# A fused mLSTM, mixture-of-experts and gated-MLP kernel: the first expert's second layer for 256 rows moved ahead of a branch, and one read-back issued an expert earlier

## The chip, the cores and the metric

The kernel runs on one core of a Trainium2 chip. The metric is the device time of one execution in microseconds (us), taken as the median of several runs. Each engine of the core has its own instruction stream and works in order: TensorE (PE in the rows, its weight loads PEld) multiplies into PSUM, VectorE (DVE) and ScalarE (ACT) work element by element, GpSimd (POOL) does the same and issues the indirect transfers, SyncE (SP) issues all other DMAs. Engines wait for one another by semaphores.

## The reference, cut to what matters

```python
def _moe_ref(x, expert_emb, tau, w1, w2):            # x: 3072 tokens x 320, from the mLSTM
    expert_idx = np.argmax(logits, axis=1)            # one of 8 experts for each token
    gate_w = probs[np.arange(N), expert_idx]
    for e in range(E):
        mask = expert_idx == e
        h = np.maximum(x[mask] @ w1[e], 0.0)          # 320 -> 1024
        out[mask] = gate_w[mask, None] * (h @ w2[e])  # 1024 -> 320

def _moe2_ref(x, w_in, w_out):
    h = x @ w_in                                      # 320 -> 2048
    g = h * (1.0 / (1.0 + np.exp(-1.702 * h)))
    return g @ w_out                                  # 2048 -> 320
```

Ahead of it stands a recurrence over 768 time steps for 4 x 8 heads (`_attn_ref`), whose output, 3072 rows of 320 values, is `x` above.

## The kernel before, in words

The kernel has three phases on one core.

**Recurrence (about 0 to 195 us).** The 768 steps are cut into chunks of 128, and each of the 24 units (batch, chunk) becomes a few matmuls. As tokens come out, they are routed: each row is scattered to a slot of its expert in the DRAM tensor `rows`. The expert with most tokens so far is named early (`first`), its weights are loaded, and at the end of the phase the first 256 of its rows (`EARLY`) go through its first layer for the first six slices of 128 hidden units (`early_mm`, `early_relu`, `WA = 6`). The result of slice m is kept in `he[m]` as a high and a low part, in a buffer of the weight ring.

**A branch.** `order` computes on VectorE how many tokens each expert has, the order of the experts and a flag, which says whether any expert has more rows than its capacity, or the first one fewer than 256 among the early rows. Every engine loads the flag into a register (`values_load`, L1389) and takes `tc.If` (L1390). Where the flag is set, `general()` does the odd cases; with these inputs it is skipped. An engine that skips the block waits for its own semaphore to reach its count at the block's entry and then adds what the block would have added (the semaphore instructions on L1390). Behind the branch, work that touches what the block could have touched waits for those counts.

**Experts (about 199 to 412 us).** Each of the 8 experts, in order of size, is 8 slices (`m`) of 128 hidden units; `s` counts the 64 steps. A step runs the first layer of its slice (`h_mm`: eight matmuls with up to 512 columns, since operands are split into a high and a low part), `relu_split` (ScalarE the high part `hh`, VectorE the low part `hl`), and then the second layer of the slice before it (`tail` -> `o_mm`: three matmuls of 320 columns for each tile of 128 rows, accumulated in `acc`; those that need `hl`, one for each tile, come last). In the last slice of an expert (`m = 7`) the order is tile by tile, so `hl` is wanted by the third matmul. The step also splits a later weight slice (`split_w`: ScalarE L105 and L118, GpSimd L110, VectorE L111 and L121), transposes the next expert's rows (`prep_x`, `prep_x0` for the first expert) and advances the conversion of the gated MLP's weights, which arrive as 64-bit floats (`convert(n)` takes `n` steps of `cvt`: L1160, L1164, L1166, L1168, L1170 on VectorE). For the first expert, `prep_x0(1, c)` makes the rows 256 to 511 ready at once behind the branch, and `prep_x0(0, c)` the rows 0 to 255 in the steps 1 to 3, because slices 6 and 7 need them; in its steps 0 to 5 `h_mm` has 256 columns only, and `he[m]` supplies the other half. When an expert is done, `put` writes its rows to the DRAM tensor `y`.

**Gated MLP (about 412 to 772 us).** Blocks of 512 sorted rows are read back from `y` (`load_y`), scaled by the gate (`scale_y`), and go through both layers. The buffer `xr` that `load_y` fills has one copy, which the experts' rows use too. The first block's read-back is issued in the last expert's step `m == 1`, `scale_y` stands on VectorE at `m == 3`, and the transposes of the block at `m = 4` to `6`.

The order on every engine is that of the program text (`tc.manual_schedule()`); SyncE issues its DMAs in that order too, and one that has to wait holds all behind it.

Of the kernel before, what the change touches and what calls it, by code (L numbers as in the profile page):

```python
# [9 lines left out]
F32 = mybir.dt.float32  # L10
# [4 lines left out]
ALU = mybir.AluOpType  # L15
# [4 lines left out]
P = 128  # L20
CAP = 512

EARLY = 256
# [3 lines left out]
def kernel(ctx, tc, qT_in, kT_in, kvo_in, i_gate, f_gate, expert_emb, tau, w12, wio, out, dbg=None):  # L27

    nc = tc.nc
    B, H, S = i_gate.shape  # L30
    NT, DM = out.shape
    D = DM // H
    E = expert_emb.shape[0]
# [13 lines left out]
    RS = NT + GN  # L47
# [957 lines left out]
    with ExitStack() as mctx:  # L1005
# [16 lines left out]
        def load_x0(j):  # L1022

            if j:
                xr_t["first"] = xp.tile([P, NB, 3 * P], F32, tag="xr", name="xr", bufs=1)
                t = xr_t["first"][:, 0:NB // 2]
            else:
                t = mp2.tile([P, NB, DM], F32, tag="o", name="xr", bufs=1).rearrange("p i d -> p (i d)")
                t = t[:, 0:NB // 2 * 3 * P].rearrange("p (i d) -> p i d", d=3 * P)
            xr_t["first", j] = t  # L1030
            src = rows[ds(ids[0] * RS + j * EARLY, EARLY), :].rearrange("(i p) d -> p i d", p=P)
            nc.sync.dma_start(out=t[:, :, 0:DM], in_=src)

        def load_x(p):
            n = CAPS[p] // P
            xr_t[p] = xp.tile([P, NB, 3 * P], F32, tag="xr", name="xr", bufs=1)
            src = rows[ds(ids[p] * RS, CAPS[p]), :].rearrange("(i p) d -> p i d", p=P)
            nc.sync.dma_start(out=xr_t[p][:, 0:n, 0:DM], in_=src)
            nc.sync.dma_start(out=xr_t[p][:, 0:n, DM:3 * P], in_=src[:, :, 2 * P:DM])
# [45 lines left out]
        def halves(hh, hl):  # L1085
            return [(hh[:, i:i + P], hl[:, i:i + P]) for i in range(0, hh.shape[-1], P)]

        def relu_split(key, out=None):
            hp = hp_t.pop(key)
            nb = hp.shape[-1]  # L1090
            hh, hl = out or (mp2.tile([P, CAP], F32R, tag="hh", name="hh")[:, 0:nb], mp2.tile([P, CAP], F32R, tag="hl", name="hl")[:, 0:nb])
            nc.scalar.activation(out=hh, in_=hp, func=AF.Relu)  # L1092
            nc.vector.scalar_tensor_tensor(out=hl, in0=hp, scalar=0.0, in1=hh.bitcast(F32), op0=ALU.max, op1=ALU.subtract)  # L1093
            hs_t[key] = halves(hh, hl)
# [11 lines left out]
            nc.vector.tensor_tensor(out=hl, in0=g, in1=hh.bitcast(F32), op=ALU.subtract)  # L1106
            hs_t[key] = halves(hh, hl)

        def o_mm(blk, key, w, first, last):
            hs = hs_t.pop(key)  # L1110
            if first:
                acc_t[blk] = [ps_a.tile([P, DM], F32, tag="acc", name="acc") for _ in range(ncol(blk) // P)]


            n = ncol(blk) // P
            order_ = [(i, j) for i in range(n) for j in range(2)] + [(i, 2) for i in range(n)]
            for i, j in sorted(order_) if last else order_:
                hh, hl = hs[i]
                nc.tensor.matmul(acc_t[blk][i], hl if j == 2 else hh, w[:, DM:2 * DM] if j == 1 else w[:, 0:DM],  # L1119
                                 start=(first and j == 0), stop=(last and j == 2))  # L1120

        def out_tile(blk):
            o = mp2.tile([P, NB, DM], F32, tag="o", name="o", bufs=1)
# [113 lines left out]
        def load_y(blk):  # L1237
            n = ncol(blk)
            xg = xp.tile([P, NB, 3 * P], F32, tag="xr", name="xr", bufs=1)[:, 0:n // P]
            src = y[row0(blk):row0(blk) + n, :].rearrange("(i p) d -> p i d", p=P)  # L1240
            nc.sync.dma_start(out=xg[:, :, 0:DM], in_=src)
            nc.sync.dma_start(out=xg[:, :, DM:3 * P], in_=src[:, :, 2 * P:DM])
            xr_t[blk] = xg
# [42 lines left out]
            nc.scalar.copy(xh_t[blk][:, c, js], x)  # L1286
            nc.vector.tensor_tensor(out=xl_t[blk][:, c, js], in0=x, in1=xh_t[blk][:, c, js].bitcast(F32), op=ALU.subtract)  # L1287

        def general_x(src):
            xr_t["g"] = xr_t["first"][:, NB - GN // P:NB]  # L1290
            src = src.rearrange("(i p) d -> p i d", p=P)
            nc.sync.dma_start(out=xr_t["g"][:, :, 0:DM], in_=src)
            nc.sync.dma_start(out=xr_t["g"][:, :, DM:3 * P], in_=src[:, :, 2 * P:DM])
            for c in range(3):
                prep_x("g", c)

# [56 lines left out]
            return work, nc.values_load(nwork_i[0:1], min_val=0, max_val=NWK)  # L1353

        def general():
            general_x(rows[ds(ids[0] * RS, EARLY), :])
            for m in range(WA):
                h_mm("g", ("g", m), wslot[m][0])
                relu_split(("g", m), he[m])
                hs_t.pop(("g", m))  # L1360
            work, nwork = general_list()
            with tc.For_i(0, nwork, 1) as w:
                zero = mp2.tile([P, 3 * P], F32, tag="fr", name="zero")[:, 0:DM]
                nc.vector.memset(zero, 0.0)
                wt = mp2.tile([1, 4], I32, tag="wt", name="wt", bufs=1)
                nc.sync.dma_start(out=wt, in_=work[ds(w, 1)])
                e, r0, r1, y0 = (nc.values_load(wt[0:1, i:i + 1], engines=sp, min_val=0, max_val=m)
                                 for i, m in enumerate([E - 1, E * RS - GN, E * RS - GN, NT + CAP - GN]))
                nc.sync.dma_start(out=rows[ds(r1, GN), :].rearrange("(i p) d -> p i d", p=P), in_=zero.unsqueeze(1).to_broadcast([P, GN // P, DM]))
                general_x(rows[ds(r0, GN), :])  # L1370
                for m in range(0, M1, 2):
                    r = mp2.tile([P, 3 * P + DM, 2], I32, tag="c", name="c")
                    r1_, r2_ = w_dma(e, m // 2, r.bitcast(F32).rearrange("p w two -> p (w two)"))
                    for i in range(2):
                        split_w1(win[:, m + i], r1_[:, :, i * P:(i + 1) * P])
                        split_w2(wout[:, m + i], r2_[:, i])
                for m in range(M1):
                    h_mm("g", ("g", m), win[:, m])
                    relu_split(("g", m))
                    o_mm("g", ("g", m), wout[:, m], m == 0, m == M1 - 1)  # L1380
                for i, o in out_tile("g"):
                    pass
                nc.sync.dma_start(out=y[ds(y0, GN), :].rearrange("(i p) d -> p i d", p=P), in_=o[:, 0:GN // P])
# [2 lines left out]
        sp = [mybir.EngineType.SP]  # L1386
        with tc.manual_schedule():
            load_x0(1)
            flag = nc.values_load(vals_i[0:1, 2 * E:2 * E + 1], min_val=0, max_val=1)  # L1389
            with tc.If(flag > 0):  # L1390
                general()
# [26 lines left out]

            def tail(p):
                e, m, s = p  # L1420
                o_mm(e, ("a", s), wslot.pop(s)[1], m == 0, m == M1 - 1)
                if m == M1 - 1:
                    put(e)

            for e, m, s in steps:
                h_mm(e, ("a", s), wslot[s][0], EARLY if s in he else 0)
                relu_split(("a", s))
                if s in he:
                    hs_t["a", s] = halves(*he.pop(s)) + hs_t["a", s]
                if prev:  # L1430
                    tail(prev)
                prev = (e, m, s)
                if 1 <= s < 4:
                    prep_x0(0, s - 1)
                if s == 1:
                    gts = gates_1()
                if s == 2:
                    gates_2(*gts)
                if s == 3:
                    order_rows()  # L1440
                if s == 4:
                    meta_tile()

                for w in [] if s == 0 else [s + WA - 1] if s < WA else [s + WA - 1, s + WA] if s == WA else [s + WA]:
                    if w < NS1:
                        split_w(w)
                        if w % 2 and w // 2 + 3 < NS1 // 2:
                            load_w(w // 2 + 3)
                if e + 1 < E and 2 <= m - (e == 0) < 5:
                    prep_x(e + 1, m - 2 - (e == 0))  # L1450
                if m == 5 + (e == 0) and e + 2 < E:
                    load_x(e + 2)
                if s % 2 == 0 and 0 <= s // 2 - 3 < NTILE:
                    meta_put(s // 2 - 3)
                if s == 7 + 2 * NTILE:
                    meta_get()
                if s == 9 + 2 * NTILE:
                    meta_split()
                if e == E - 1:

                    if m == 1:
                        load_y(E)
                    if m == 3:
                        scale_y(E, nc.vector)
                    if 4 <= m < 7:
                        prep_x(E, m - 4)
                    if m == 7:
                        load_y(E + 1)

                if s > 3:  # L1470
                    convert((1 if CAPS[e] < CAP else 2) + (m % 4 > 0))

            def tail2(p):
# [102 lines left out]
```

## Time and profile before

| | |
|---|---|
| median of 3 runs | 773.79 us (773.63 to 774.51) |
| the profiled execution, its own time | 774.2 us |
| its span, first to last instruction | 772.5 us |
| mean granted TensorE clock | 0.985 |
| TensorE busy (matmuls) | 726.2 us, 94% of the span |
| VectorE, ScalarE, GpSimd busy | 560.0, 354.3, 248.0 us |

The 1.7 us between the span and the execution's own time lie around the span and are not part of the program. Busy matmul time is modelled and overlaps, so that 94% says that TensorE is seldom without work and not how fast it works. A granted clock of 1 is TensorE's upper level, 2.4 GHz, and one of 0.5 its lower, 1.2 GHz; a mean in between is a mix of both. Times in the rows are microseconds from the span's start.

### The profile page before, as it was taken

To read this page: it belongs to the slowest core of one execution; us is meant where nothing else is said; L and a number is where in the kernel's file an instruction comes from. 1 tells how busy PE (TensorE), PEld (TensorE's weight loads), DVE (VectorE), ACT (ScalarE), POOL (GpSimd) and SP (SyncE) were. 2 spreads that over 40 slices of the span, in tenths; PEclk is the share of its full clock that TensorE was granted. 3 is DMA by queue.
4 is the path that set the end of the run, shared out by engine and by line. 5 is a ranking of instruction groups with operands and counts; after the bars stand their busy time and mean duration, and the time that the engine had idled before them with its cause. 6 is when DMAs were issued, how large, how long until landed. Compare 5 with 4: busy or idle time off the path is not lost.

```text
span 772.5 us, 13249 instructions
## 1 busy us (share of the span) xinstructions
PE 726.2 (94%) x4708; PEld 678.3 (88%) x4708; DVE 560.0 (72%) x1146; ACT 354.3 (46%) x834; POOL 248.0 (32%) x362
## 2 busy tenths in 40 slices
PE   6798988879899999999989999999999999999995
PEld 6697988778889999999988888889889889989994
DVE  8888999998599989999977785554554554445542
ACT  4353424414465666666744554343333343334442
POOL 5564476785233434454511002002002002002011
PEclk9899999999999999999999999999999999999998
DMA  6979887752657765778633220120120110101000
GB/s 206 304 252 302 273 249 242 236 180 98 226 145 234 225 185 181 187 187 265 179 105 105 59 62 34 31 52 35 29 54 34 28 36 26 50 1 40 17 18 17
DMA packets 70302, 100.19 MB, mean 130 GB/s; under 512 B 31120, under 2 KB 56472, under 8 KB 70232
## 3 DMA queue, kind: packets, MB, share of 16 engines
q1 hardware_dynamic: 67160, 91.41, 39.9%
q0 software_dynamic: 3072, 7.89, 2.7%
q8 instruction: 38, 0.62, 0.4%
q14 instruction: 32, 0.26, 0.1%
HBM read 77.53 MB, written 17.82 MB: 123 GB/s over the span
## 4 chain that ended last, share of the span: by engine, by line
PE 45%; issue 20%; DVE 5%; POOL 2%; ACT 1%; POOLq 0%; ACTq 0%; DVEq 0%
PE hp L138 22%; PE acc L1119 21%; POOL out_dram L1141 2%; DVE w L121 1%; PE xt L1053 1%; DVE hl L1093 1%; POOL xr L1247 1%; DVE w L111 1%; DVE ex L1160 0%; DVE xl L1055 0%; DVE fr L1170 0%; DVE es L1168 0%; DVE sg L1104 0%; DVE fr L1166 0%; DVE hhl L1106 0%
## 5 line engine op out<-in xcount | busy, mean ns | idle before, releaser
L1119 PE MATMUL acc<-wout,hhl 128*128 128x320 f32 x1152 | 187.5, 310 | 0.1
L1119 PEld LDWEIGHTS acc<-wout,hhl 128*128 128x128 f32 x1152 | 175.9, 188 | 7.9 <-ACT o L1128 0.3
L1104 DVE TENSOR_TENSOR sg<-hp,sg 128x512 f32<-128x512 f32 (+1 forms) x112 | 68.7, 614 | 88.4 <-ACT sg L1103 88.3
L138 PE MATMUL hp<-xh,win 128*128 128x512 f32 (+1 forms) x560 | 131.1, 364 | 0.0
L1106 DVE TENSOR_TENSOR hhl<-sg,hhl 128x512 fp32r<-128x512 f32 (+1 forms) x112 | 71.4, 637 | 70.0 <-ACT hhl L1105 70.0
L1103 ACT ACTIVATE sg<-hp 128x512 f32<-128x512 f32 (+1 forms) x112 | 60.2, 538 | 115.4 <-PE hp L138 115.2
L1141 POOL DMA_INDIRECT out_dram<-o,tokd x24 | 24.0, 1000 | 273.6 <-ACT o L1128 269.9
L1105 ACT CAST hhl<-sg 128x512 fp32r<-128x512 f32 (+1 forms) x112 | 62.6, 559 | 91.0 <-DVE sg L1104 91.0
L138 PEld LDWEIGHTS hp<-xh,win 128*128 128x128 f32 x560 | 93.9, 188 | 11.5 <-ACT xh L1286 0.2
L138 PE MATMUL hp<-xl,win 128*128 128x512 f32 (+1 forms) x336 | 85.7, 363 | 0.0
L110 POOL TENSOR_TENSOR w<-r,w 128x256 fp32r<-128x256 f32 x58 | 46.4, 800 | 107.0 <-ACT w L105 106.6
L138 PE MATMUL hp<-xh,w 128*128 128x384 f32 (+2 forms) x320 | 75.7, 368 | 0.2 <-ACT xh L1070 0.2
L1119 PE MATMUL acc<-w,hh 128*128 128x320 f32 x424 | 75.6, 309 | 0.0
L1119 PEld LDWEIGHTS acc<-w,hh 128*128 128x128 f32 x424 | 67.7, 188 | 2.3
L138 PEld LDWEIGHTS hp<-xl,win 128*128 128x128 f32 x336 | 58.9, 189 | 10.8 <-DVE xl L1287 0.2
L360 DVE TENSOR_TENSOR_SCAN pm<-fb,ident_h 128x1024 f32<-128x1024 f32 x23 | 56.7, 2464 | 5.2 <-DMA fb<-dec 5.1
L400 PE MATMUL sp<-qT,kblk 120*128 120x128 f32 x384 | 50.8, 288 | 10.1 <-DVE wm L405 10.1
L400 PEld LDWEIGHTS sp<-qT,kblk 120*128 120x128 f32 x384 | 46.9, 200 | 14.7 <-DVE wm L405 12.7
L138 PEld LDWEIGHTS hp<-xh,w 128*128 128x128 f32 x320 | 55.1, 193 | 4.0 <-ACT xh L1070 0.4
L1092 ACT ACTIVATE hh<-hp 128x384 fp32r<-128x384 f32 (+2 forms) x64 | 33.5, 524 | 44.8 <-PE hp L138 43.8
L138 PE MATMUL hp<-xl,w 128*128 128x384 f32 (+2 forms) x192 | 47.9, 358 | 0.0
L1119 PE MATMUL acc<-w,hl 128*128 128x320 f32 x212 | 44.9, 310 | 1.5 <-DVE hl L1093 1.3
(305 smaller groups left out, 1219.2 us busy)
## 6 DMA issues: line engine op xcount, KB each, us to landing
r<-in_w_dram SPq DMA_DIRECT2D x32, 704.0 KB
fb<-dec SPq DMA_DIRECT2D x23, 512.0 KB
kvo<-in_kvo_dram SPq DMA_DIRECT2D x24, 480.0 KB
c<-in_wio_dram SPq DMA_DIRECT2D x16, 704.0 KB
rows<-zt SPq DMA_DIRECT2D x8, 640.0 KB
qT<-in_qT_dram SPq DMA_DIRECT2D x24, 180.0 KB
xr<-y SPq DMA_DIRECT2D x5, 640.0 KB
kblk<-in_kT_dram SPq DMA_DIRECT2D x48, 60.0 KB
```

The costliest lines, as they stand in the source:

```text
L110: eng.tensor_tensor(out=t[:, 3 * P:5 * P].rearrange("p (c f) -> p c f", c=2), in0=r1[:, 0:2], in1=hif[:, 0:2], op=ALU.subtract)
L111: nc.vector.tensor_tensor(out=hi[64:P, 2], in0=r1[64:P, 2], in1=hif[64:P, 2], op=ALU.subtract)
L138: nc.tensor.matmul(hp, a, b, start=(i == 0), stop=(i == len(seq) - 1))
L360: nc.vector.tensor_tensor_scan(out=pm[u].rearrange("p h t -> p (h t)"), data0=fb[u].rearrange("p h t -> p (h t)"), data1=ident_h.rearrange ...
L400: nc.tensor.matmul(sp[:, h - hs.start], kblk[u % NLD][0:KR, h // 3, h % 3, :], qT[u][0:KR, h // 3, :], start=True, stop=True)
L1092: nc.scalar.activation(out=hh, in_=hp, func=AF.Relu)
L1103: nc.scalar.activation(out=sg, in_=hp, func=AF.Sigmoid, scale=1.702)
L1104: nc.vector.tensor_tensor(out=g, in0=hp, in1=sg, op=ALU.mult)
L1105: nc.scalar.copy(hh, g)
L1106: nc.vector.tensor_tensor(out=hl, in0=g, in1=hh.bitcast(F32), op=ALU.subtract)
L1119: nc.tensor.matmul(acc_t[blk][i], hl if j == 2 else hh, w[:, DM:2 * DM] if j == 1 else w[:, 0:DM], start=(first and j == 0), stop=(last an ...
L1141: sc = nc.gpsimd.indirect_dma_start(out=out, out_offset=bass.IndirectOffsetOnAxis(ap=tokd[:, ti:ti + 1], axis=0), in_=o[:, i], in_offset=None)
```

## The change

There are three edits.

1. Ahead of the flag's load, the accumulators of the first expert's four row tiles are allocated, and `early_o` runs the second layer for the two early tiles and the six slices of `he`: 6 x 2 x 3 = 36 matmuls of 320 columns. In the expert's steps 1 to 6, `tail` then does tiles 2 and 3 alone for these six slices, six matmuls in place of twelve. Where the flag is set, `general()` computes these rows again; `late_rows` first clears those that were already counted, so that adding is right. That block's own accumulators move to the other PSUM pool.
2. `load_y(E)`, the read-back of the gated MLP's first 512 rows, is issued in step `m == 5` of the last but one expert and no longer in step `m == 1` of the last.
3. `convert` begins in step 5 and no longer in step 4.

```diff
-        def o_mm(blk, key, w, first, last):
-            hs = hs_t.pop(key)
-            if first:
-                acc_t[blk] = [ps_a.tile([P, DM], F32, tag="acc", name="acc") for _ in range(ncol(blk) // P)]
+        def o_mm(blk, key, w, first, last, tiles=None, hs=None):
+            hs = hs or hs_t.pop(key)
+            if first and blk not in acc_t:
+                acc_tiles(blk)
...
-            n = ncol(blk) // P
-            order_ = [(i, j) for i in range(n) for j in range(2)] + [(i, 2) for i in range(n)]
+            tiles = tiles or range(len(acc_t[blk]))
+            order_ = [(i, j) for i in tiles for j in range(2)] + [(i, 2) for i in tiles]
...
+        def acc_tiles(blk):
+            n = -(-ncol(blk) // P)
+            if blk == "g":
+                acc_t[blk] = [ps_x.tile([P, CAP], F32, tag="xt", name="acc")[:, 0:DM] for _ in range(n)]
+            else:
+                acc_t[blk] = [ps_a.tile([P, DM], F32, tag="acc", name="acc") for _ in range(n)]
+
+        NE = EARLY // P
+
+        def early_o(m, first):
+
+            o_mm(0, None, wslot[m][1], first, False, range(NE), halves(*he[m]))
+
+        def late_rows(x):
+
+            t = mp2.tile([P, 3 * P], F32, tag="fr", name="t")[:, 0:NE]
+            nc.vector.tensor_copy(t, tok_i[:, 0:NE])
+            nc.vector.tensor_scalar(out=t, in0=t, scalar1=lack, scalar2=None, op0=ALU.is_ge)
+            nc.vector.tensor_tensor(out=x, in0=x, in1=t.unsqueeze(2).to_broadcast([P, NE, 3 * P]), op=ALU.mult)
...
         def general():
-            general_x(rows[ds(ids[0] * RS, EARLY), :])
+            general_x(rows[ds(ids[0] * RS, EARLY), :], late_rows)
...
+            for m in range(WA):
+                early_o(m, False)
...
             load_x0(1)
+            acc_tiles(0)
+            for m in range(WA):
+                early_o(m, m == 0)
             flag = nc.values_load(vals_i[0:1, 2 * E:2 * E + 1], min_val=0, max_val=1)
             with tc.If(flag > 0):
                 general()
...
-                o_mm(e, ("a", s), wslot.pop(s)[1], m == 0, m == M1 - 1)
+                o_mm(e, ("a", s), wslot.pop(s)[1], m == 0, m == M1 - 1, range(NE, len(acc_t[0])) if s < WA else None)
...
                 if m == 5 + (e == 0) and e + 2 < E:
                     load_x(e + 2)
+                if m == 5 and e + 2 == E:
+                    load_y(E)
...
-                    if m == 1:
-                        load_y(E)
...
-                if s > 3:
+                if s > 4:
                     convert((1 if CAPS[e] < CAP else 2) + (m % 4 > 0))
```

## Rows read from the trace of the kernel before

**Rows 1.** TensorE's timeline around the branch: start, us, operation, count [idle before <-releaser].

```profile
194.99 0.52 PE L138 MATMUL hp<-xel,w 128*128 128x256 f32 x3
197.35 0.41 PE L1077 MATMUL xt<-ident 128*128 128x64 f32 x2 [1.84 <-DVEq L1390]
...
199.55 1.44 PE L138 MATMUL hp<-xh,w 128*128 128x256 f32 x5 [0.16 <-ACT xh L1070]
...
202.92 0.74 PE L1119 MATMUL acc<-w,he 128*128 128x320 f32 x4
...
204.66 0.38 PE L1069 MATMUL xt<-ident,xr 128*128 128x128 f32 x2
204.80 0.84 PE L138 MATMUL hp<-xh,w 128*128 128x256 f32 x5
...
205.84 0.75 PE L1119 MATMUL acc<-w,he 128*128 128x320 f32 x4
```

**Rows 2.** Records of the branch's line: engine, instruction, count, ns, first and last start.

```profile
L1390 SPq EVENT_SEMAPHORE  x9: 17/17/17, 196.3 to 198.6; - x9
L1390 PEldq EVENT_SEMAPHORE  x2: 51/51/51, 195.6 to 195.7; - x2
...
L1390 DVEq EVENT_SEMAPHORE  x2: 21/21/21, 197.2 to 197.3; - x2
```

**Rows 3.** SyncE's timeline: the first transfer issued behind the branch.

```profile
199.75 0.39 SPq L1032 DMA_DIRECT2D xr<-rows  x1
```

**Rows 4.** Busy time of each engine by stretch, granted clock, DMA share and GB/s.

```profile
200.00:205.00 5.00, 5.00 (x31) 5.00 (x31) 1.46 (x4) 1.00 (x4) 0.00 (x0) 0.74 0.76 234
...
210.00:215.00 5.00, 5.00 (x41) 4.99 (x40) 4.67 (x16) 3.41 (x9) 1.97 (x3) 1.00 0.69 248
215.00:220.00 5.00, 5.00 (x33) 4.63 (x32) 4.87 (x13) 3.22 (x8) 0.74 (x1) 1.00 0.44 146
```

**Rows 5.** TensorE's timeline in step 8.

```profile
228.38 0.42 PE L1119 MATMUL acc<-w,hl 128*128 128x320 f32 x1 [1.32 <-DVE hl L1093]
```

**Rows 6.** VectorE's timeline in the first expert's steps 1 to 7.

```profile
205.49 0.42 DVE L1071 TENSOR_TENSOR xl<-xt,xh 128x256 fp32r<-128x256 f32 x1 [1.48 <-ACT xh L1070]
...
208.34 0.29 DVE L111 TENSOR_TENSOR w<-r,w 64x128 fp32r<-64x128 f32 x1 [0.83 <-ACT w L105]
...
214.47 0.49 DVE L121 TENSOR_TENSOR w<-r,w 128x320 fp32r<-128x320 f32 x1
...
216.41 1.07 DVE L121 TENSOR_TENSOR w<-r,w 128x320 fp32r<-128x320 f32 x1
...
220.78 1.10 DVE L1168 SCALAR_TENSOR_TENSOR es<-c,es 128x384 int32<-128x384 int32 x1
...
226.26 0.29 DVE L111 TENSOR_TENSOR win<-fr,win 64x128 fp32r<-64x128 f32 x1
226.56 0.33 DVE L1160 TENSOR_SCALAR ex<-c 128x320 int32<-128x320 int32 x1
...
227.64 0.68 DVE L1093 SCALAR_TENSOR_TENSOR hl<-hp,hh 128x512 fp32r<-128x512 f32 x1
```

**Rows 7.** TensorE's timeline in the last expert.

```profile
402.07 0.63 PE L1053 MATMUL xt<-ident,xr 128*128 128x128 f32 x4 [1.96 <-issue]
```

**Rows 8.** TensorE's timeline in the recurrence: an idle time under a full clock.

```profile
172.19 0.22 PE L588 MATMUL r<-oh_all,ones 128*128 128x24 bf16 x3 [1.62 <-DVE oh_all L568]
```

**Rows 9.** GpSimd's timeline in step 4.

```profile
216.39 0.74 POOL L110 TENSOR_TENSOR w<-r,w 128x256 fp32r<-128x256 f32 x1 [2.31 <-ACT w L105]
```

**Rows 10.** SyncE's timeline in the last two experts.

```profile
384.20 0.38 SPq L1231 DMA_DIRECT2D metat<-meta  x1
390.49 0.40 SPq L1136 DMA_DIRECT2D y<-o  x1
395.24 0.38 SPq L1241 DMA_DIRECT2D xr<-y  x1
```

**Rows 11.** VectorE's timeline in the last expert.

```profile
400.21 1.76 DVE L1247 TENSOR_TENSOR xr<-xr,gated 128x1536 f32<-128x1536 f32 x1 [2.97 <-DMA xr<-y]
```

More of the change, by code (lines that the diff above doesn't have):

```diff
@@ L1287, in parts, with general_x @@
             nc.vector.tensor_tensor(out=xl_t[blk][:, c, js], in0=x, in1=xh_t[blk][:, c, js].bitcast(F32), op=ALU.subtract)
-        def general_x(src):
+        def general_x(src, keep=None):
             xr_t["g"] = xr_t["first"][:, NB - GN // P:NB]
@@ L1293, in general_x @@
             nc.sync.dma_start(out=xr_t["g"][:, :, DM:3 * P], in_=src[:, :, 2 * P:DM])
+            if keep:
+                keep(xr_t["g"])
             for c in range(3):
@@ L1379, in general @@
                     relu_split(("g", m))
+                    if m == 0:
+                        acc_tiles("g")
                     o_mm("g", ("g", m), wout[:, m], m == 0, m == M1 - 1)
```

## Prediction

> **What bounds the kernel now.** The page says 94% for TensorE over the whole span, which does not say where a saving would count. So I read TensorE's timeline and looked for its idle times after the recurrence. There are three.
>
> The first is the branch. The last matmuls ahead of it start at 194.99 and are done at 195.51. The first layer of the first expert starts at 199.55, so 4.04 us pass, in which TensorE has only a touch at 197.35 and six transposes [rows 1]. The records of the branch's line say what it waits for: VectorE adds its count at 197.2, and SyncE has its last count, which needs the landing of the rows 256 to 511, at 198.6 [rows 2]. SyncE's next transfer goes out at 199.75 [rows 3].
>
> At the same place the clock falls. In 200 to 205 us the granted clock averages 0.74, a mix of the half level (1.2 GHz) and the full one (2.4 GHz) [rows 4], after a stretch with hardly any matmuls. Two first-layer slices take 3.37 us there (199.55 to 202.92); the next slice takes 1.04 (204.80 to 205.84) [rows 1].
>
> The second idle time is in step 8: 1.32 us for `hl`, from VectorE [rows 5]. It is the sign of a stretch that TensorE does not set. In 210 to 220 us VectorE is busy for 4.67 and 4.87 of each 5 us [rows 4], and its timeline from 208.34 to the `hl` at 227.64 has no idle time of note [rows 6]. What comes earlier on TensorE here is worth nothing unless VectorE comes earlier too. From step 8 to the end of the last expert TensorE is back to back, and VectorE has a little room.
>
> The third is 1.96 us at 402.07, in the last expert [rows 7].
>
> **Edit 1, the second layer ahead of the branch.** It moves 36 matmuls of 320 columns; nothing is added. Twelve take 1.74 us (202.92 to 204.66) [rows 1], so 36 take 5.2. Their inputs are there: `he` is finished slice by slice with the first layer ahead of them, and six matmuls of each slice leave its last operation 0.87 us. Three matmuls right before took 0.52 us, the full rate [rows 1], so they run from 195.4 to about 200.8.
>
> TensorE's count for the branch now comes at 200.85 in place of 195.6 [rows 2], later than VectorE's and SyncE's. What follows on TensorE has nothing of theirs left to wait for: from the end of its work to the touch about 0.46 us (195.51 to the second record at 195.7, and an issue), to the transposes 0.3, and from those to the first layer 1.06, as before. That is 1.8 in place of 4.04. The bounds of this gap are 1.3 (all issued behind the matmuls, with the transposes' way through ScalarE alone left) and 4.04 (the old gap again). I take 1.8, nearest to the steps that the rows show, since what filled the rest was over by 198.6. The first layer then starts at 202.65, 3.1 later than before. The clock should stay up: an idle time of 1.62 us at 172 left it full [rows 8], and here some 0.5 and 0.6 us are idle between touch, transposes and first layer. The two slices then take about 2.3 us (2 x 1.04 and a short wait for the transposed rows' low parts) in place of 3.37, and the first `tail` six matmuls, 0.87, in place of 1.74.
>
> So the first transposes of the rows 0 to 255, at 204.66 before [rows 1], come 3.1 - 1.07 - 0.87 = **1.2 us later** (0.7 to 3.4 by the gap's bounds). On them VectorE's full stretch hangs: its `xl` at 205.49 waits for ScalarE's copy of these transposes, and behind it in its queue stand the gates, then the weight splits from 208.34 [rows 6]. That all of it shifts by 1.2 is what edit 1 costs; the 0.87 us that TensorE saves in each of steps 2 to 6 lie beside VectorE and gain nothing.
>
> SyncE's transfers: 199.75 [rows 3] stands behind TensorE's count and becomes about 201.5. That shifts nine transfers (the rows 0 to 255, two weight loads, the next expert's rows in two parts, two chunks of the MLP's weights, then two more weight loads) and fifteen register loads by 1.75. The rows 0 to 255 had landed when their transposes ran at 204.66, after 4.9 us at most, so they are there by 206.4 at the latest, and likely by the 205.8 at which they are wanted. The others are wanted in steps 3 to 8, behind VectorE's queue, which comes later itself. GpSimd has no work there. I cost these at nothing; without that cover it would be 0.6 for the first and 1.75 for the rest, inside the upper bound above.
>
> **Edit 3, the conversion a step later.** Two conversion steps leave VectorE's full stretch and come back in the MLP's first block, where VectorE has room. Before the `hl` at 227.64 stand eight steps; six will stand there. What falls out is three of the four operations between 226.26 and 227.64 (L1160 stays): 1.38 - 0.33, some 1.1 us [rows 6]. The order shifts by two as well, so the operation of 1.10 us at 220.78 and the one behind it may meet GpSimd or not. A split of 320 columns took 0.49 us at 214.47 and 1.07 at 216.41, as GpSimd's subtraction began at 216.39 [rows 6, 9]; two such meetings less save 1.1 more. So edit 3 saves 1.1 to 2.2; I take 1.7, the middle, since either is as near.
>
> The Trainium skill bears on this (SBUF — State Buffer, section Who interferes with whom): a VectorE instruction with both inputs in SBUF and a GpSimd instruction that reads SBUF shut each other out, and the one that starts first holds on to its end. By that rule, the trace agrees with 1.07 against 0.49 us. It speaks against this change, as an engine that runs ahead puts GpSimd's work under other VectorE instructions.
>
> Both together: `hl` of step 7 comes 1.2 - 1.7 = **0.5 us earlier** (bounds: 0.7 - 2.2 = -1.5 and 3.4 - 1.1 = +2.3). TensorE is there some 0.6 us earlier than before without the waits, so it still waits for this `hl`, and from there on all is as before, 0.5 us earlier. Edit 2 has its own room.
>
> **Edit 2, the read-back.** Before, SyncE issues `put` of the last but one expert at 390.49, and the read-back at 395.24, as it waits for that write to land [rows 10]. VectorE's scaling waits 2.97 us for the data, until 400.21, and takes 1.76 [rows 11]; the transposes start as it ends, 1.96 us late [rows 7]. After, the read-back stands in step 5 of the last but one expert, ahead of that `put`. It then waits for the write of the expert before, issued five steps earlier, and for the buffer `xr`, free with the step before. Behind it in the queue stand the transfer at 384.20 [rows 10], which waits for its own data anyway, and the `put`, which now waits for the read-back: the read-back took 5.0 us (395.24 to 400.21), and from 379 that is 384, well before 390. The scaling starts at 397.24, as VectorE comes to it, and is done at 399.0; TensorE wants it at 400.1. So **1.96 us** go, with 1.1 to spare for the next `hl`. The bounds are 0 and 1.96; no wait is in sight to take its place, so I take 1.96.
>
> **Sum.** The profiled execution took 774.2 us, 772.5 of span and 1.7 around it; it becomes 774.2 - 0.5 - 1.96 = 771.7. The median of the runs is 0.4 below that execution, so the forecast is 773.8 - 2.5 = **771.3 us**. A change under 0.2%, 1.55 us, can't be told from none.
>
> **The rivals.**
> - *TensorE sets the pace.* If VectorE is not what holds steps 1 to 8, TensorE keeps its own gain: 5.2 moved, 1.07 by the clock, less 3.1, that is 3.2, and the 1.32 wait. With edit 2, 6.5: 767.3 us. For it speaks that TensorE has no idle time until step 8; against it that VectorE has none either, with fixed work. Chance 0.15, mostly in between, from 770 down.
> - *The branch's gap comes again*, behind the second layer: +3.4, -1.7 and -1.96 make 773.5 us, no change. More meetings with GpSimd, at 0.58 each, would do the same. Against it: its waits were for what is long past by then [rows 2]. 0.12.
> - *The read-back still comes late*, because SyncE is held, or another wait follows at the same place: 773.3 us. The write to `y` and the buffer speak against it. 0.08.
> - *Slower: the early second layer runs at the half clock.* A matmul would take 0.27 us (3.37 over 16 of 256 columns, scaled to 320), the 36 of them 4.5 more. That puts VectorE's stretch 5.7 late: 5.7 - 1.7 - 1.96 makes 775.8 us. With 20 of the 36 slow the change is even, with 32 it is slower by 0.2%. The full rate right before speaks against it, so 0.05.
>
> **How the numbers follow.** The forecast has 0.60, of which 0.02 falls within 0.2%; its own range is 770.3 to 772.4. Faster by over 0.2%: 0.58 + 0.15 = 0.73. Within: 0.02 + 0.12 + 0.08 = 0.22. Slower: 0.05. The range from 769.6 to 773.5 takes in the upper bound of the first stretch with edit 2, and leaves out the slow case and the better part of the first rival, under 0.2.
>
> **What would show it.** Right: the 36 matmuls on TensorE from 195.4 to 200.8; a full clock in 200 to 205; the first transposes of rows 0 to 255 at about 205.8, and VectorE full from 209 to 227; waits of TensorE for `hl` in steps 3 to 8; no idle time ahead of the block's first transposes. Wrong: those transposes clearly before 204.7 or after 207, `hl` of step 7 before 226 or after 228.5, or a new wait in the last expert.

## The result, and the profile after

The changed kernel takes 779.26 us (median of seven runs, 775.85 to 779.84) against 773.79 for the kernel before on the same chip: the ratio is 1.0058, with a 95% interval of 1.0044 to 1.0071. It is 5.5 us slower, where 2.5 us less were forecast. The profiled execution took 779.84 us with a span of 778.1.

TensorE's timeline around the branch, of the changed kernel (columns as in [rows 1], which it answers; L1077 is the touch, one small matmul ahead of the transposes; PEq and PEldq are the queues in which TensorE takes its instructions in order):

```profile
197.05 0.51 PE L138 MATMUL hp<-xel,w 128*128 128x256 f32 x3
198.50 5.54 PE L1119 MATMUL acc<-w,he 128*128 128x320 f32 x36 [0.93 <-DVE he L751]
208.14 0.66 PE L1077 MATMUL xt<-ident 128*128 128x64 f32 x2 [4.10 <-PEq L1419]
208.59 1.49 PE L1069 MATMUL xt<-ident,xr 128*128 128x128 f32 x6
209.80 1.44 PE L138 MATMUL hp<-xh,w 128*128 128x256 f32 x5
...
213.37 0.76 PE L1119 MATMUL acc<-w,hh 128*128 128x320 f32 x4
213.97 0.46 PE L1119 MATMUL acc<-w,hl 128*128 128x320 f32 x2
214.26 0.38 PE L1069 MATMUL xt<-ident,xr 128*128 128x128 f32 x2
...
218.59 0.85 PE L1119 MATMUL acc<-w,hh 128*128 128x320 f32 x4 [0.96 <-ACT hh L1092]
```

The 36 matmuls run at the full rate and end at 204.04. Then TensorE is idle for 4.10 us, and what it waits for is its own queue at the branch's line. From 204.04 to the first layer at 209.80 pass 5.76 us; the forecast had 1.8. The first transposes of the rows 0 to 255 come at 214.26, 16.7 us after the end of the early first layer (197.56); before it was 9.15 (195.51 to 204.66) [rows 1].

The records of the branch's line in the changed kernel, as in [rows 2] (ns between the slashes):

```profile
L1419 SPq COMPARE_BRANCH  x1: 50/50/50, 197.3 to 197.3; - x1
L1419 POOLq COMPARE_BRANCH  x1: 45/45/45, 197.6 to 197.6; - x1
L1419 ACTq COMPARE_BRANCH  x1: 50/50/50, 198.1 to 198.1; - x1
L1419 DVEq COMPARE_BRANCH  x1: 72/72/72, 198.7 to 198.7; - x1
L1419 PEldq COMPARE_BRANCH  x1: 5752/5752/5752, 201.9 to 201.9; - x1
```

and the one for TensorE in the kernel before:

```profile
L1390 PEldq COMPARE_BRANCH  x1: 445/445/445, 195.1 to 195.1; - x1
```

The branch instruction itself takes 5.75 us on TensorE's queue, and 0.45 before. The four other engines take it in 0.07 or less. What TensorE does meanwhile is in the transfers: the DMA queues of the changed kernel from 201.9 to 205.2 us (first line), and from 205.2 to 207.7:

```profile
q1 hardware_dynamic: 282, 0.88, 75.3%
```

```profile
q8 instruction: 1, 0.02, 2.4%
q1 hardware_dynamic: 2, 0.00, 0.1%
```

While the branch stands, SyncE's queue (q1) moves 0.88 MB; as it falls silent, one packet of instructions comes over q8. By the trace it starts at 205.27, takes 0.97 us, and the branch is over at 207.60.

The stretches, as in [rows 4]:

```profile
200.00:205.00 5.00, 4.04 (x28) 3.77 (x26) 0.06 (x1) 0.00 (x0) 0.00 (x0) 1.00 0.65 210
205.00:210.00 5.00, 1.86 (x9) 1.73 (x10) 0.22 (x1) 0.62 (x2) 0.00 (x0) 0.65 0.03 8
210.00:215.00 5.00, 5.00 (x30) 4.99 (x30) 1.79 (x5) 1.71 (x6) 0.00 (x0) 0.67 0.73 205
```

Behind the 4.10 us the granted clock is 0.65 and 0.67, a mix of the half level (1.2 GHz) and the full one. The two first slices take 3.57 us (209.80 to 213.37). VectorE, the engine on which the next stretch hangs, does 0.28 us of work in ten.

SyncE's timeline, which answers [rows 3] and the first of [rows 10]:

```profile
199.98 0.39 SPq L1032 DMA_DIRECT2D xr<-rows  x1
201.23 0.35 SPq L96 DMA_DIRECT2D r<-in_w_dram  x1
210.22 0.37 SPq L1038 DMA_DIRECT2D xr<-rows  x1
...
385.82 0.39 SPq L1261 DMA_DIRECT2D xr<-y  x1
...
398.05 0.39 SPq L1156 DMA_DIRECT2D y<-o  x1
```

The rows 0 to 255 go out at 199.98, not held by the 36 matmuls; the next expert's rows do wait for TensorE and go out at 210.22. The read-back now stands 12 us ahead of the last write. In the last expert VectorE and TensorE show (as in [rows 11] and [rows 7]):

```profile
404.18 1.75 DVE L1267 TENSOR_TENSOR xr<-xr,gated 128x1536 f32<-128x1536 f32 x1
```

```profile
406.96 0.60 PE L1053 MATMUL xt<-ident,xr 128*128 128x128 f32 x4
```

Neither waits any more. This part went as forecast.

### The profile page after: what moved, and what is told of

It reads as the page before. It is cut to its first block, busy times and chain, and to the rows that moved or that the text cites. A ratio compares the mean times of both kernels' runs of the same rounds, so it can differ in the third digit from the quotient of the medians.

```text
span 778.1 us, 13252 instructions
## 1 busy us (share of the span) xinstructions
PE 729.8 (94%) x4708; PEld 681.1 (88%) x4708; DVE 558.8 (72%) x1146; ACT 353.9 (45%) x834; POOL 246.1 (32%) x362
## 4 chain that ended last, share of the span: by engine, by line
issue 36%; PE 25%; DVE 6%; POOL 4%; ACT 2%; POOLq 0%; DVEq 0%; ACTq 0%
PE hp L138 12%; PE acc L1119 11%; POOL out_dram L1161 3%; POOL xr L1267 1%; PE xt L1053 1%; ACT hhl L1105 1%; DVE hhl L1106 1%; DVE sg L1104 1%; DVE es L1188 0%; DVE ex L1180 0%; DVE w L121 0%; DVE fr L1190 0%; DVE xt L1289 0%; POOL gap L1163 0%; DVE hl L1093 0%
## 5 line engine op out<-in xcount | busy, mean ns | idle before, releaser
L400 PE MATMUL sp<-qT,kblk 120*128 120x128 f32 x384 | 53.4, 297 | 9.3 <-DVE wm L405 9.3
L400 PEld LDWEIGHTS sp<-qT,kblk 120*128 120x128 f32 x384 | 49.8, 210 | 13.6 <-DVE wm L405 11.8
```

Source lines behind the costliest of these rows:

```text
L400: nc.tensor.matmul(sp[:, h - hs.start], kblk[u % NLD][0:KR, h // 3, h % 3, :], qT[u][0:KR, h // 3, :], start=True, stop=True)
```

## The experiments

All twelve were timed beside the kernel before, whose median was 774.1 to 774.3 us. A TensorE instruction's place below is counted in the compiled program: four for a matmul with a float32 operand, two for another, one for all else. (In the trace the touch, one float32 matmul of the program text, leaves two matmuls and two weight loads.) The kernel before has its branch at 3044 and the target, behind the skipped block, at 3461; the changed one has 3116 and 3604. The first theory (A) was that the target is not among the instructions that TensorE holds and has to be fetched. Its rivals were that the moved matmuls (B) or the two small edits (C) cost the time.

### 1. A shorter block to skip

```diff
 (the changed kernel)
-            for m in range(WA):
-                early_o(m, False)
             work, nwork = general_list()
```

> The changed kernel without the second layer of the early rows in the skipped block (72 TensorE instructions fewer to jump over; the flagged case, which these inputs do not take, loses that part of its result). Theory A, the branch's target has to be fetched: TensorE's branch stands at instruction 3116 of its program as in the change, its target moves from 3604 to 3532, that is from page 14.08 to page 13.80 in pages of 256 instructions; if the page after the branch's own is held already, the branch takes 0.4 to 0.5 us in place of 5.75, the touch comes about 5.3 us earlier, the clock's low stretch behind it shortens, the load of block 1's rows no longer waits 8.2 us, and the time is 772.5 us (771.0 to 774.5). Rival B, the 36 moved matmuls and their late start cost the time: the skipped block is never run, so nothing changes, branch near 5.75 us or the time at 779 (778 to 780). Rival C, the shifted convert and the early read-back cost it: also 779.

Measured: 777.72 us, ratio 1.0047 (1.0031 to 1.0064). The time can't be told from that of the change and is far from 772.5, but the branch is shorter:

```profile
L1417 PEldq COMPARE_BRANCH  x1: 3932/3932/3932, 201.5 to 201.5; - x1
```

Branch 3116, target 3532: still a fetch. A's guess of where the held part ends was wrong. The jump here is 416 instructions long, and in the kernel before, with 0.445 us, it is 417; so the length of the jump is not what decides.

### 2. The kernel before, with more to skip

```diff
 (the kernel before, in general())
+            for m in range(WA * 6):
+                touch()
             work, nwork = general_list()
```

> The kernel before with 36 float32 matmuls (144 TensorE instructions) added to the skipped block alone; nothing that runs on these inputs changes. Theory A: the branch stays at instruction 3044 (page 11.89), its target moves from 3461 (13.52) to 3605 (14.08); the page has to be fetched, the branch takes 5 to 6 us in place of 0.445, and the time is 779 us (777.5 to 780.5). Rivals B and C: nothing that runs has changed, the branch takes 0.445 us and the time is 773.8 (773.3 to 774.5).

Measured: 775.17 us, ratio 1.0005 (0.9993 to 1.0016).

```profile
L1392 PEldq COMPARE_BRANCH  x1: 3623/3623/3623, 197.5 to 197.5; - x1
```

```profile
201.62 0.66 PE L1077 MATMUL xt<-ident 128*128 128x64 f32 x2 [3.64 <-PEq L1392]
```

Instructions that never run make TensorE's branch eight times as long: that is A's mechanism with nothing of the change in it. The packet of instructions starts 1.07 us after the branch. The time hardly shows the stall, which A had not expected. The idle time ahead of the touch grows from 1.84 [rows 1] to 3.64 only, since without the fetch TensorE waits there anyway. In this execution the read-back cost TensorE nothing (see 8), which offsets that; why the other executions show so little is open. In the change the stall begins behind the 36 matmuls, when all other waits are over, and counts in full.

### 3. The two small edits alone

```diff
 (the kernel before)
+                if m == 5 and e + 2 == E:
+                    load_y(E)
...
-                    if m == 1:
-                        load_y(E)
...
-                if s > 3:
+                if s > 4:
                     convert((1 if CAPS[e] < CAP else 2) + (m % 4 > 0))
```

> The kernel before with the read-back's earlier issue and the shifted convert alone, without the early second layer. Theory A: branch and clock as before; the wait of 1.96 us at the last expert goes and up to some 0.5 us of waits in step 7: 771.5 us (770.8 to 772.2). Rival C, one of these two edits costs time: 774.5 or more.

Measured: 770.86 us, ratio 0.9945 (0.9925 to 0.9966). C is out: these edits are the change's gain.

### 4. The early second layer behind the branch

```diff
 (the changed kernel; the additions inside the skipped block go too)
-            acc_tiles(0)
-            for m in range(WA):
-                early_o(m, m == 0)
             flag = ...
             with tc.If(flag > 0):
                 general()
+            acc_tiles(0)
+            for m in range(WA):
+                early_o(m, m == 0)
             touch()
```

> The whole change with the early second layer placed behind the branch, ahead of the touch (in the flagged case the early rows' first layer is made anew inside the block, so nothing has to be added there); skipped block and branch stand where they stood before, 3044 and 3461. Theory A: the branch takes 0.445 us, the 36 matmuls run behind it at the full clock and fill the idle time ahead of the touch and the first layer, and the time is 771.0 us (769.5 to 772.5). Rival B, the 36 moved matmuls cost the time wherever they stand: 776 or more.

Measured: 773.51 us, ratio 0.9987 (0.9975 to 0.9998); the branch takes 0.445 us. The stall is gone and with it most of the loss, but the kernel is 2.65 us slower than the one without early matmuls. So B holds for a part. TensorE's waits in this kernel from 198 to 260 us (us in total, times, longest):

```profile
PE acc L1119 <- DVE hl L1093: 1.4, 2, 0.9
PE acc L1119 <- ACTq L1414: 1.1, 1, 1.1
PE acc L1119 <- ACT hh L1092: 0.9, 1, 0.9
```

VectorE's timeline in it, from the first weight split to the `hl` of step 6, the first of 512 columns:

```profile
212.02 0.29 DVE L111 TENSOR_TENSOR w<-r,w 64x128 fp32r<-64x128 f32 x1 [0.83 <-ACT w L105]
...
224.61 0.68 DVE L1093 SCALAR_TENSOR_TENSOR hl<-hp,hh 128x512 fp32r<-128x512 f32 x1
```

and in the kernel of experiment 3:

```profile
210.19 0.29 DVE L111 TENSOR_TENSOR w<-r,w 64x128 fp32r<-64x128 f32 x1 [0.83 <-ACT w L105]
...
222.81 0.69 DVE L1093 SCALAR_TENSOR_TENSOR hl<-hp,hh 128x512 fp32r<-128x512 f32 x1
...
227.46 0.68 DVE L1093 SCALAR_TENSOR_TENSOR hl<-hp,hh 128x512 fp32r<-128x512 f32 x1
```

The chain to the `hl` of step 6 takes the same 12.6 us in both, without idle time. But with the early layer its start stands 14.6 us behind the end of the early first layer (197.42), without it 11.7 (198.50), and 11.7 to 12.8 in the five profiles that have neither early matmuls nor a fetch. TensorE is ready sooner in each step and waits for a VectorE that starts 1.8 to 2.9 us later. That is theory E of the runs below.

### 5. The changed kernel with its target held

```diff
 (the changed kernel, in general())
-            for m in range(WA):
-                h_mm("g", ("g", m), wslot[m][0])
-                relu_split(("g", m), he[m])
-                hs_t.pop(("g", m))
-            for m in range(WA):
-                early_o(m, False)
```

> The changed kernel with the early rows' first and second layer left out of the skipped block (168 TensorE instructions fewer to jump over; the flagged case, which these inputs do not take, loses that part). Branch at instruction 3116 as in the change, its target at 3436 in place of 3604. Theory A, sharpened by the first four runs (branch 3044 and target 3461: 0.445 us, twice; 3044 and 3605: 3.62; 3116 and 3532: 3.93; 3116 and 3604: 5.75): what counts is where the target stands, and the page that is held ends somewhere between 3461 and 3532, so 3436 is held: the branch takes 0.4 to 0.5 us, TensorE goes from the 36 matmuls to the touch with less than 0.3 us idle, and the time is that of the early layer behind the branch, 773.5 us (772.3 to 774.7). Rival, any target behind TensorE's later branch has to be fetched: the branch takes 3.5 us or more and the time is 776 or more.

Measured: 773.85 us, ratio 0.9998 (0.9988 to 1.0007).

```profile
L1413 PEldq COMPARE_BRANCH  x1: 353/353/353, 201.3 to 201.3; - x1
```

```profile
197.97 5.55 PE L1119 MATMUL acc<-w,he 128*128 128x320 f32 x36 [0.93 <-DVE he L751]
203.96 0.41 PE L1077 MATMUL xt<-ident 128*128 128x64 f32 x2 [0.45 <-PEq L1413]
204.21 0.88 PE L1069 MATMUL xt<-ident,xr 128*128 128x128 f32 x6
205.17 0.94 PE L138 MATMUL hp<-xh,w 128*128 128x256 f32 x5
```

Nothing that runs on these inputs differs from the changed kernel, and 5.4 us are gone. With the target at 3436 the branch takes 0.353 us, the idle time is 0.45 us, the first layer comes 1.65 us behind the matmuls, and the clock stays at 1.00. In the change the gap is 5.76, 4.1 more, and the half clock costs the two first slices 1.3 (3.57 against 2.28, 205.17 to 207.45 here): together the 5.4.

### 6. The weights out of the fetch's way

```diff
 (the changed kernel)
-                    load_w(WA // 2 + 1)
                     for c in range(3):
                         prep_x0(1, c)
                     load_x(1)
+                    load_w(WA // 2 + 1)
```

> The changed kernel with the load of the next two slices' weights issued behind the load of block 1's rows in place of ahead of it; branch and target stand as in the change (3116 and 3604). Theory D, the fetch waits behind the weights' packets: in the change it starts 3.4 us after the branch, when SyncE's packets end; without the weights in its way it starts 1.0 to 1.7 us after the branch, the branch takes 3.4 to 4.0 us in place of 5.75, and the time is 777.0 us (775.5 to 778.3). Rival, a fetch two pages on is 5.75 us by itself: 5.5 to 6.0 us, and 779.

Measured: 776.18 us, ratio 1.0023 (1.0011 to 1.0035).

```profile
L1419 PEldq COMPARE_BRANCH  x1: 3832/3832/3832, 201.8 to 201.8; - x1
```

With target and branch where the change has them, the fetch starts at 203.30, 1.5 us after the branch in place of 3.4, and the branch takes 1.9 us less. In all four kernels with a fetch the branch ends 2.3 to 2.6 us after the fetch starts (207.60 - 205.27 in the change); what differs is how long it takes to start. That the weights' transfer delays it is not shown: in experiment 1, with the weights where the change has them and their packets under way, it also started 1.6 us after the branch (203.12). What made it 3.4 in the change's profile is left open. The time is some 3 us below the change's, and the two intervals do not meet; but the move also lets the next expert's rows go out sooner (207.93, 210.22 in the change), so not all of it need be the branch.

### 7. Two slices' matmuls in place of six

```diff
 (the kernel of experiment 4)
-            for m in range(WA):
+            for m in range(2):
                 early_o(m, m == 0)
...
-... range(NE, len(acc_t[0])) if s < WA else None)
+... range(NE, len(acc_t[0])) if s < 2 else None)
```

> The kernel with the early read-back and the shifted convert, and of the early second layer only slices 0 and 1 (12 matmuls, 1.8 us) behind the branch. Theory E, the 36 matmuls cost 2.6 us because they stand ahead of the first transposes, with VectorE idle for 4.9 us of 200 to 205 and then the bound: 12 matmuls fit nearly into TensorE's idle 1.85 us ahead of the touch and hold VectorE up by 1.0 us at most; the clock stays full. Expected 770.2 us (769.0 to 771.5), not above the 770.86 of the kernel without early matmuls by more than 0.5. Rival, early matmuls cost by their number: a third of 2.65, 771.7.

Measured: 771.11 us, ratio 0.9957 (0.9944 to 0.9970). 12 matmuls cost nothing that can be told; they gain nothing either against experiment 3. The interval does not exclude the rival's 771.7, but the trace speaks for E: VectorE's first weight split stands 11.1 us behind the early first layer here (209.81 - 198.75), no later than without early matmuls.

### 8. The convert's shift alone

```diff
 (the kernel before)
-                if s > 3:
+                if s > 4:
```

> The kernel before with the convert's start shifted by one step alone; read-back and early layer as before. Together with the early read-back it was 3.4 us (0.55%) faster than before. If most of that is the VectorE work taken out of steps 4 to 15: 771.6 us (770.8 to 772.5). If most of it is the read-back (1.96 us of idle TensorE in the profile before, but 0 in the padded kernel's, where the last write of the expert's rows landed in 2.7 us and not 4.7): 773 or more.

Measured: 775.06 us, ratio 1.0004 (0.9992 to 1.0017): a miss. TensorE's wait for `hl` in step 8 [rows 5] is gone from the trace, but in the last expert stands

```profile
401.41 0.71 PE L1053 MATMUL xt<-ident,xr 128*128 128x128 f32 x4 [2.32 <-DVE xr L1247]
401.80 1.93 PE L138 MATMUL hp<-xh,w 128*128 128x384 f32 x5
```

What the convert gives is there, and most of it is lost again. Counted from the end of the early first layer, TensorE comes to this wait 3.3 us sooner than in the profile before (201.3 us, 204.6), of which 1.0 was gained ahead of the transposes of the rows 0 to 255. The wait is then 0.4 longer; from it to the gated MLP's first matmul pass 11.1 us in place of 9.5, as the granted clock is 0.64 in the first 4.8 us behind the wait (1.00 before); and from that matmul to the end 361.7 in place of 360.9 (see below on edit 3). Of the 3.3 us 0.5 are left.

The read-back itself waits for the landing of the write ahead of it, here 4.60 us after the write was issued (390.01 to 394.61). SyncE's timeline of experiment 2, in the same expert, has

```profile
394.73 0.40 SPq L1136 DMA_DIRECT2D y<-o  x1
397.47 0.38 SPq L1241 DMA_DIRECT2D xr<-y  x1
```

2.74 us, where the profile before had 4.75 [rows 10], and TensorE did not wait at all. The 1.96 us of [rows 7] are one draw of a wait that was between 0 and 2.3 in three profiles.

### 9 to 12. VectorE's work lightened, and the read-back alone

Three kernels move nine parts of the convert, some 5 us of VectorE, from steps 5 to 7 into the last expert: that of experiment 4 (36 early matmuls), of 7 (12) and of 3 (none).

```diff
-                if s > 4:
-                    convert((1 if CAPS[e] < CAP else 2) + (m % 4 > 0))
+                if s > 7:
+                    convert((1 if CAPS[e] < CAP else 2) + (m % 4 > 0) + (s > 54))
```

> The early second layer behind the branch, with the convert's first nine parts (three steps' worth, some 5 us of VectorE at 0.3 to 1.1 us each) moved from steps 5 to 7 into the last expert, where VectorE is busy 15.8 of 20 us. Theory E: VectorE is the bound in steps 2 to 8 of that kernel (its chain from the first weight remainder to the first 512-wide hl takes 12.6 us with and without the early layer, and starts 2.9 us later with it). Lightening it gives back TensorE's waits for hl of 1.4 us: 772.3 us (771.4 to 773.0). Rival, TensorE is held by something else there: 773.5 as before.

> The kernel with two slices' early matmuls behind the branch (771.11) and the same nine parts of the convert moved. Theory E: TensorE is busy without a gap in steps 2 to 15 of that kernel (its waits behind the branch come to 0.4 us), so taking work from VectorE gives next to nothing: 770.8 us (770.2 to 771.4). Rival, VectorE is the bound with two early slices too: 769.7 or less.

> The kernel with the early read-back and without an early second layer (770.86), with the same nine parts of the convert moved from steps 5 to 7 into the last expert: the control for the two kernels with early matmuls, which the move took from 773.51 to 771.89 (36 early matmuls) and from 771.11 to 770.30 (12). Theory E: without early matmuls TensorE has no wait in steps 1 to 15, so the move gives nothing: 770.9 us (770.2 to 771.6). Rival, the move is worth 1 us or more by itself whatever TensorE waits for: 769.8 or less.

The fourth run, which follows, is the kernel before with the first two parts of experiment 3's diff only: edit 2 alone.

> The kernel before with the read-back's earlier issue alone. By TensorE's wait in the profile before: 1.96 us, 772.2 us (771.5 to 773.0). By the two runs with the convert shifted, with and without the early read-back, whose last seven experts took 179.3 and 183.3 us: up to 4.0 us, 770.3. If the read-back gave nothing by itself: 774.

| early matmuls | as in 4, 7, 3 | VectorE lightened (ratio to the kernel before) | gain |
|---|---|---|---|
| 36 | 773.51 | 771.89 (0.9947 to 0.9977) | 1.6 |
| 12 | 771.11 | 770.30 (0.9933 to 0.9964) | 0.8 |
| none | 770.86 | 770.42 (0.9932 to 0.9966) | 0.4 |

The gain falls with the number of early matmuls, as E has it; the last two gains are within the spread of the runs, and the first is at its edge. With 36, TensorE's two waits for `hl` become one (0.9 us, of 1.4). The kernel stays 1.5 us behind the one without early matmuls (771.89, 770.42), so E is shown for a part of the loss only. What is left in its trace are that wait for `hl` and one of 0.9 us for `hh`, neither of which the kernel without early matmuls has. Read-back alone: 770.95 us, ratio 0.9955 (0.9940 to 0.9970). The fastest kernels stand at 770.3 to 771.1 and can't be told apart; the simplest of them has edit 2 alone.

## Why the prediction was wrong

By the medians: edit 2 gives 3.3 us (774.26 to 770.95), edit 3 on top of it 0.1, not to be told from nothing or from 1.5 (770.86); the early second layer costs 2.65 to 3.0 (773.51, 773.85), and the fetch at the branch 5.4 (779.26). That is 4.7 to 5.0 slower; measured are 5.5. In the two profiled executions 2.05 of the difference lies ahead of all this, in the recurrence, where the early first layer ended at about 195 to 198.7 us in the fourteen profiles, with early matmuls or without.

- **The step that failed** is the gap behind the early matmuls: "1.8 in place of 4.04", with "4.04 (the old gap again)" as the upper bound. Measured were 5.76. The 1.8 is right where the target is held (1.65 in experiment 5). But the branch was taken over at its old price, while the edit put 72 TensorE instructions ahead of it and 71 more into the block it skips. An old gap bounds a new one only if the same things end it. That 0.445 us on TensorE stood against 0.045 to 0.072 on the others was there to see in the same view as [rows 2]. The rival that the gap comes again came nearest in size, but it had the old waits as its cause, and those were over. The Trainium skill has the rule (Runtime: NRT & Kernel Launch, section Instruction fetch mechanics): a taken branch whose target is not in the two pages that are held has to wait until the page is fetched. Experiments 1, 2 and 5 agree, with 3.93 and 3.62 us against 0.353; how much is held, no run here shows.
- **The clock** was to stay full; it does in experiments 4 and 5 and fell in the change only behind the 4.10 us, which made the two first slices 1.3 us longer. The slow rival was right in sign and wrong in place: the 36 matmuls ran at the full rate (5.54 us, forecast 5.2).
- **Their start** at 195.4, straight behind the early first layer: it came 0.93 us later, as the first of them waits for VectorE's last `he` though it reads only the first slice.
- **VectorE's stretch** was named as what edit 1 moves, 1.2 us later (0.7 to 3.4). In experiment 5 the transposes of the rows 0 to 255 come 11.3 us behind the early first layer (208.34 - 197.04) in place of 9.15: 2.15 later, 0.9 of it the late start. The mechanism was right, the term too small; against the rival that TensorE sets the pace there speak experiment 4, where the early layer costs time without a stall, and, less strongly, experiment 9.
- **Edit 3** was to save 1.7 us of VectorE (1.1 to 2.2), and it did: from the first weight split to the `hl` of step 7 pass 17.3 us in experiment 3 (210.19 to 227.46) and 19.3 before (208.34 to 227.64) [rows 6], 2.0 less, and the wait of [rows 5] is gone where the edit stands without the early layer. What failed is that the two conversion steps "come back in the MLP's first block, where VectorE has room", at no cost. In the gated MLP of the changed kernel TensorE waits twice, at 424.18 in the first block and at 474.57 as the second begins:

```profile
PE acc L1119 <- ACT o L1148: 0.4, 1, 0.4
PE hp L138 <- ACT xh L1306: 0.2, 1, 0.2
```

All eleven profiles with the shift have these two waits, and from the MLP's first matmul to the end of the span they take 361.7 to 361.8 us. The three without it have none there and take 360.9 to 361.0. So 0.7 to 0.8 us go back; why ScalarE is late there was not followed. TensorE gains more than that before: from the transposes of the rows 0 to 255 to those of the read-back pass 193.1 us in experiment 3 and 195.3 in 11. Some 1.5 us would remain of it, which the times are too coarse to show.

- **Edit 2**: the wait went, with time to spare, as forecast; measured alone it is worth 3.3 us (2.3 to 4.6), above the bound of 1.96, which came from one execution of a wait that varies. It can cost the clock as well: in experiment 8 the five matmuls behind it took 1.93 us, the half clock, in the profile before 1.11. It cost 1.6 us there, up to the MLP's first matmul. Whether that makes up all of the 3.3 is not settled.
- **SyncE's transfers**: the first was not shifted by 1.75; the one behind the weights was, by 8.4 (210.22, 201.78 before). No wait of VectorE or TensorE for it shows behind the stall.

## What to carry to other kernels

Ahead of a conditional, count what an edit adds to each engine's instructions before and inside the skipped block, and read the duration of the branch itself for every engine: a branch whose target has to be fetched took TensorE 3.6 to 5.75 us here, against 0.35 to 0.45, and padding or a shorter block moves a kernel over that edge although none of it runs. Work that fills one engine's gap is only worth moving if it does not stand ahead of what feeds the next bound; here 36 matmuls that ran for free beside a busy VectorE were moved ahead of it and let it start 1.8 to 2.9 us later. Work that is shifted off a full stretch has to be priced where it lands: two conversion steps cost TensorE 0.7 to 0.8 us in a stretch that was taken to have room. A wait for a transfer is a draw: before a saving is taken from one profile, look at what the wait would have been on another.

## What was not expected of the hardware

- The length of the jump does not set the branch's price: 417 instructions on took 0.445 us, 416 on took 3.93, with both places 71 to 72 instructions later. If one edge holds for both places of the branch, it lies between 3461 and 3532 in this program; where exactly was not tried.
- The idle time alone does not say whether the clock falls. In experiment 1, 2.22 us of it behind the 36 matmuls left the clock full; in experiment 6, 2.11 us behind the same matmuls did not. Their stretches from 205 to 210 us:

```profile
205.00:210.00 5.00, 4.00 (x29) 3.58 (x30) 1.51 (x4) 1.66 (x6) 0.00 (x0) 1.00 0.31 86
```

```profile
205.00:210.00 5.00, 3.92 (x20) 3.80 (x21) 1.16 (x3) 1.35 (x4) 0.00 (x0) 0.66 0.18 32
```

- The read-back went out 2.74 us behind the write of 480 KB that it waits for in one execution, and 4.75 behind it in another at the same place.
